# Splitting the scale weights by columns and reordering the text work in a dual-stream attention block

## Chip, cores and metric

The kernel runs on one core of a Trainium2 chip. The metric is the device time of one execution in microseconds. Weights and activations are bfloat16, sums float32.

## The reference

Two streams share one attention: 2 x 256 image tokens and 2 x 32 text tokens of width D = 1152. A conditioning vector c gives each stream a shift, a scale and a gate.

```python
mod_i = (_silu(c) @ wmod_img).reshape(B, 6, 1, D)      # likewise mod_t from wmod_txt
shi, sci, gai = mod_i[:, 0], mod_i[:, 1], mod_i[:, 2]
hi = _layernorm(x_img) * (1 + sci) + shi
ht = _layernorm(x_txt) * (1 + sct) + sht
qkvi, qkvt = hi @ wqkv_img, ht @ wqkv_txt              # each cut into q, k, v of width D
q, k, v = (concatenate([text, image], axis=1) ...)
p = _softmax(einsum('bqd,bkd->bqk', q, k) * D ** -0.5)
a = einsum('bqk,bkd->bqd', p, v)                       # one head of width D
at, ai = a[:, :Nt], a[:, Nt:]
out_i = x_img + gai * (ai @ wo_img)
out_t = x_txt + gat * (at @ wo_txt)
```

Of the six parts of each modulation, the first three are used. With all weights, the kernel reads 39.5 MB.

## The kernel before

**Tiles and loads.** A weight matrix of 1152 x 1152 lies in SBUF as nine blocks of 128 rows (`KT` = 9). Five slots hold such matrices; a slot is loaded again once its last reader is done. SP's queue issues nearly all loads in the program's order: x, the image scale weights `w_sc_i` by rows 0-3, 4-6, 7, 8 (line 108), the V weights `w_v_i` by rows (line 110), shift, q, text shift, k, text scale, text q and k. Behind the k stage's third hook come the late loads (`late_loads`, line 567): the image gate, the shift's V rows, text V, wo_img in two parts, the text gate, wo_txt in three. `pin` keeps instructions in the order in which the program gives them, on their engine; all matmuls go through `mm` (line 61), all PE transposes through `tr` (line 64).

**The head.** While weights arrive, c goes through silu into the columns `sT`, and TensorE runs warm-up matmuls (`warm_up`). ScalarE sums two of the four image tiles of 128 tokens (`ln_sums`), VectorE takes the statistics of the other two (`ln_stats`). The normalised tiles `xn_i` are transposed on TensorE in groups of three row blocks into PSUM tiles `tp`, which `x_out` copies into `xT_i`. The image scale is formed twice: `sc_rows` makes all of it as rows, four column groups beside each other, in matmuls of 288 columns, and `sc_cols` transposes them on VectorE; `sc_first` makes block 0 as columns, with the weights as stationary operand and `sT` as two moving columns. `x_scale` writes the scaled `hS_i` block by block.

**V.** `v_open` accumulates V over the nine row blocks, 512 columns at a time: `A0` is batch 0, `A1` the first half of batch 1, and the keys (2, 1) and (3, 1) the rest. The order before is: blocks 0-2 of A0, blocks 0-2 of A1, blocks 3-6 of both, blocks 7-8 key by key, then (2, 1), the shift rows (`mod_rows_of`), then (3, 1), and the last 128 columns (`v_last`). V is computed from the scaled tokens; the part of V that comes from the shift (`shift_v_rows`) is added behind the attention.

**q, k and text.** VectorE and ScalarE apply scale and shift to `xT_i` (lines 357-364, then called `hT_i`). `qk_img` makes q and k: for each of nine column blocks j it accumulates nine matmuls of 512 columns, and ahead of chosen j it runs hooks with the text work. The text shift is summed on VectorE (`shift_part`, line 450).

**Attention and output.** Four score tiles for the image and one for the text, then the image gate (`img_gate`), then text V (`v_txt`), with the softmax on VectorE, ScalarE and GpSimd beside them. `p_transposes` transposes P on TensorE. `gate_row` sends the gate's rows to HBM and `img_gate_spread` brings them back to all partitions as `gb`. `out_img` makes one image tile of the output in chunks of 384 columns: nine matmuls, then VectorE multiplies by the gate (line 723) and adds x (line 724). Behind tile 1 come the text gate (`txt_gate`) and the text output (`out_txt`), behind tile 2 the text products and sums (`out_txt_store`, lines 746 and 747):

```python
    out_img(1, C3)
    txt_gate()
    txt = out_txt()
    out_img(2, C3)
    out_txt_store(txt)
    out_img(3, (CH, CH, 224, 160), parts=(2 * CH, D - 160, D))
```

Of the kernel before, what the change touches and what calls it, by code (L numbers as in the profile page):

```python
# [14 lines left out]
def kernel(  # L15
# [14 lines left out]
    nc = tc.nc  # L30
# [75 lines left out]
    SCC = (0, 4, 7, K8, KT)  # L106
    for r0, r1 in zip(SCC, SCC[1:]):
        nc.sync.dma_start(w_sc_i[:, r0:r1, :], sc_v[:, r0:r1, :])  # L108
    for r0, r1 in ((0, 1), (1, 2), (2, 3), (3, 5), (5, 7), (7, KT)):
        nc.sync.dma_start(w_v_i[:, r0:r1, :], v_v[:, r0:r1, :])  # L110
    w_sh_i = load_w(2, wmod_img, 0)
    w_q_i = load_rows(3, wqkv_img, 0)
    w_sh_t = load_rows(0, wmod_txt, 0, (0, 1, 3, 6))
# [10 lines left out]
    nc.vector.memset(warm[:], 1.0)  # L124
    NGG = 4
# [7 lines left out]
    def warm_up(n):  # L133
        for _ in range(n):
            mm(wps[:], lhsT=warm[:, 0:P], rhs=warm[:], start=True, stop=True)

    warm_up(8)
# [27 lines left out]
    warm_up(14)  # L165
# [15 lines left out]
    def ln_stats(x_ap, np_, between=None):  # L181
        stats = small.tile([P, NCH, 6], f32, tag="stats")
        for k in range(NCH):
            if k == 1 and between:
                between()
            pin(nc.vector.bn_stats(stats[0:np_, k, :], x_ap[:, k * CH:(k + 1) * CH]))
        mv = small.tile([P, 2], f32, tag="mv")
        pin(nc.vector.bn_aggr(mv[0:np_, :], stats[0:np_, :, :]))
        return mv
# [34 lines left out]
    sc0_ps = ps_mm.tile([P, B], f32, tag="mm")  # L224
    tp60 = ps_mm.tile([P, 3, NI], bf, tag="mm", name="tp")
    tp61 = ps_mm.tile([P, 3, NI], bf, tag="mm", name="tp")
    sc_ps = ps_mm.tile([P, KT, LW], f32, tag="mm")

    def sc_first(r0, r1):
        if r0 == 0:  # L230
            mm(sc0_ps[:], lhsT=warm[:, 0:P], rhs=unit[:, 0:B], start=True, stop=False)
        for kt in range(r0, r1):
            mm(sc0_ps[:], lhsT=w_sc_i[:, kt, 0:P], rhs=sT[:, kt, :], start=False, stop=(kt == KT - 1))

    def sc_rows(r0, r1):
        if r0 == 0:
            for g in range(NGG):
                mm(sc_ps[LW * g:LW * g + LW].rearrange("p c l -> p (c l)"), lhsT=unit[:], rhs=warm[:, 0:KT * LW],
                   start=True, stop=False, tile_position=(0, LW * g))
        for kt in range(r0, r1):  # L240
            for g in range(NGG):
                mm(sc_ps[LW * g:LW * g + LW], lhsT=sT32[:, kt, :], rhs=group(w_sc_i, kt, g),
                   start=False, stop=(kt == KT - 1), tile_position=(0, LW * g))

    def x_tiles(k0, b):
        return (tp61 if b else tp60) if k0 == 6 else ps_tr.tile([P, 3, NI], bf, tag="tr", name="tp")

    def x_transposes(tp, k0, b, ts=range(TPB)):
        for kt in range(k0, k0 + 3):
            for t in ts:  # L250
                i = b * TPB + t
                tr(tp[:, kt - k0, t * P:(t + 1) * P], xn_i[:, i, kt * P:(kt + 1) * P], ident[:])

    def x_out(tp, k0, b):
        dst = xT_i[:, k0:k0 + 3, b * NI:(b + 1) * NI]
        pin(nc.vector.tensor_copy(dst, tp[:]) if k0 == 3 else nc.scalar.copy(dst, tp[:]))

    sc1_i = const.tile([P, KT, LW], f32, name="scc", tag="scc")

    def sc_cols(c0, c1):  # L260
        pin(nc.vector.transpose(sc1_i[:, c0:c1, :].rearrange("p c l -> p (c l)"),
                                sc_ps[:, c0:c1, :].rearrange("p c l -> p (c l)")))

    def x_scale(k0, k1, b, step=TPB, first=False):
        for kt in range(k0, k1):
            for t in range(0, TPB, step):
                t0, t1 = b * NI + t * P, b * NI + (t + step) * P
                pin(nc.vector.tensor_scalar(hS_i[:, kt, t0:t1], xT_i[:, kt, t0:t1],  # L268
                                            sc0_ps[:, b:b + 1] if first else sc1_i[:, kt, b:b + 1], None,
                                            op0=ALU.mult))  # L270
# [27 lines left out]
    m1 = ln_stats(x_i[:, 1, :], P, between=silu_cols)  # L298
# [3 lines left out]
    tps = [(x_tiles(k0, 0), k0, 0) for k0 in (3, 0, 6)]  # L302
    for tp in tps:
        x_transposes(*tp)
    s2 = ln_sums(x_i[:, 2, :], xn_i[:, 2, :])
    m3 = ln_stats(x_i[:, 3, :], P)
    ln_var(s2)
    x_out(*tps[0])
    r3, r2 = ln_rstd(m3[:, 1:2], P), ln_rstd(s2[:, 2:3], P, sign=-1.0)
    ln_norm(x_i[:, 3, :], m3[:, 0:1], r3, P, xn_i[:, 3, :])  # L310
    ln_norm(x_i[:, 2, :], s2[:, 0:1], r2, P, xn_i[:, 2, :])
    x_out(*tps[1])
    x_out(*tps[2])
    sc_rows(0, 4)
    sc_first(0, 4)
    warm_up(2)
    t3, t0, t6 = [(x_tiles(k0, 1), k0, 1) for k0 in (3, 0, 6)]
    x_transposes(*t3, ts=(1,))
    x_transposes(*t6, ts=(1,))
    sc_rows(4, 7)  # L320
    sc_first(4, 7)
    x_transposes(*t3, ts=(0,))
    x_transposes(*t6, ts=(0,))
    x_transposes(*t0)
    x_out(*t3)
    x_out(*t6)
    x_out(*t0)
    sc_first(7, K8)
    sc_first(K8, KT)
    sc_rows(7, KT)  # L330
    x_scale(0, 1, 0, step=1, first=True)
    sc_cols(0, 5)
    x_scale(1, 3, 0)
    v_open(A0, 0, 3)
    x_scale(0, 3, 1)
    sc_cols(5, KT)
    for k0 in (3, 6):
        for b in range(B):
            x_scale(k0, k0 + 3, b)
    v_open(A1, 0, 3)  # L340
    v_open(A0 + A1, 3, KT - 2)
# [10 lines left out]
    v_open([(2, 1)], 0, KT)  # L352
    p_sh = mod_rows_of(w_sh_i, sT32)
# [11 lines left out]
    v_open([(3, 1)], 0, KT)  # L365
# [15 lines left out]
    def qk_img(wq, blk, hooks):  # L381
        for j in range(KT):
            for hook in hooks.get(j, ()):
                hook()
            ps = ps_mm.tile([P, B * NI], f32, tag="mm")
            for kt in range(KT):
                mm(ps[:], lhsT=wq[:, kt, j * P:(j + 1) * P], rhs=hT_i[:, kt, :],
                   start=(kt == 0), stop=(kt == KT - 1))
            qk_evac(qkT[:, blk * KT + j, :, 0:NI], ps[:].rearrange("p (b n) -> p b n", b=B), blk)

    gsc = tc.dram_tile([2, B, D], bf, name="mod_scratch")
# [141 lines left out]
    def mod_row_out(gps, si):  # L533
        g_sb = work.tile([P, VC], bf, tag="garow")
        pin(nc.scalar.copy(g_sb[:], gps[:]))
        for b in range(B):
            pin(nc.gpsimd.dma_start(gsc[si, b, :].rearrange("(g j) -> g j", g=NGG), g_sb[b:P:32, :]))
# [15 lines left out]
    def txt_gate():  # L553
        mod_row_out(mod_rows(w_ga_t), 1)
        for g in range(2):
            pin(nc.gpsimd.dma_start(xf[64 * g:64 * g + NTT, :, :],
                                    xt_flat.rearrange("t (r g j) -> g t r j", r=2, g=2)[g]))
        for g in range(2):
            for b in range(B):
                r0 = 64 * g + 32 * b  # L560
                pin(nc.gpsimd.dma_start(gbf[r0:r0 + NT, :, :],
# [5 lines left out]
    def late_loads():  # L567
        late["ga_i"] = load_w(0, wmod_img, 2 * D)
        shift_v_spread()
        late["v_t"] = load_w(2, wqkv_txt, 2 * D)  # L570
# [5 lines left out]
                      5: (shift_part(4, 7),), 8: (shift_part(7, KT),)})  # L576
    qk_img(w_k_i, 1, {1: (txt_transposes,), 2: (shift_v_rows, txt_rows_scale, late_loads), 4: (shift_blocks, txt_scale),
# [100 lines left out]
    img_gate()  # L678
# [19 lines left out]
    gate_row()  # L698
# [8 lines left out]
    p_out(1, pt1, nc.scalar.copy, 1, B)  # L707
    img_gate_spread()
# [3 lines left out]
    def out_img(i, chunks, parts=None):  # L712
# [4 lines left out]
        for n in chunks:  # L717
# [33 lines left out]

    C3 = (CH, CH, CH)
    out_img(0, C3)
    out_img(1, C3)
    txt_gate()
    txt = out_txt()
# [33 lines left out]
```

## Time and profile before

| | |
|---|---|
| median of 14 runs | 117.24 us (116.55 to 119.75) |
| the profiled execution's own time | 117.85 us |
| its span | 115.8 us |
| TensorE busy | 110.1 us (95%) |
| VectorE busy | 72.3 us (62%) |
| ScalarE busy | 46.0 us (40%) |
| GpSimd busy | 13.2 us (11%) |
| moved by DMA | 41.02 MB, 354 GB/s over the span |

Times inside the kernel are counted from the span's start. In the profile PE is TensorE's matmuls, PEld its weight loads, DVE VectorE, ACT ScalarE, POOL GpSimd, SP SyncE. A line of the timeline gives start, length, engine, source line, operation, out<-in, shape and count; in brackets stands the idle time before it and what ended it. Consecutive instructions of one kind are merged, and the length of merged ones reaches from the first start to the last end. Matmuls are pipelined: each is shown some 0.16 us longer than its place in the stream. The share of busy time is a mean over stages with different limits.

### The profile page before, as it was taken

To read this page: it belongs to the slowest core of one execution; us is meant where nothing else is said; L and a number is where in the kernel's file an instruction comes from. 1 tells how busy PE (TensorE), PEld (TensorE's weight loads), DVE (VectorE), ACT (ScalarE), POOL (GpSimd) and SP (SyncE) were. 2 spreads that over 40 slices of the span, in tenths; PEclk is the share of its full clock that TensorE was granted. 3 is DMA by queue.
4 is the path that set the end of the run, shared out by engine and by line. 5 is a ranking of instruction groups with operands and counts; after the bars stand their busy time and mean duration, and the time that the engine had idled before them with its cause. 6 is when DMAs were issued, how large, how long until landed. Compare 5 with 4: busy or idle time off the path is not lost.

```text
span 115.8 us, 2644 instructions
## 1 busy us (share of the span) xinstructions
PE 110.1 (95%) x1109; PEld 63.2 (55%) x1109; DVE 72.3 (62%) x151; ACT 46.0 (40%) x97; POOL 13.2 (11%) x33
## 2 busy tenths in 40 slices
PE   4999899999999999999999999999999999999990
PEld 2245544444574444444744458887666566676670
DVE  3479494044799997999998040018758608904791
ACT  4799710032562369994323223244637500010000
POOL 7000000000000000000000000003440300068130
PEclk9999999999999999999999999999999999999999
DMA  3999999999999999999999999999999999952143
GB/s 127 369 350 382 400 401 408 416 409 410 413 405 404 319 382 409 410 409 326 395 399 408 411 404 415 351 404 408 411 405 409 408 416 409 406 205 76 26 135 120
DMA packets 18917, 41.02 MB, mean 354 GB/s; under 512 B 1323, under 2 KB 1851, under 8 KB 18907
## 3 DMA queue, kind: packets, MB, share of 16 engines
q1 hardware_dynamic: 18032, 39.85, 90.1%
q0 software_dynamic: 480, 0.89, 2.3%
q10 hardware_dynamic: 395, 0.12, 0.5%
q8 instruction: 8, 0.13, 0.4%
q14 instruction: 2, 0.02, 0.0%
HBM read 39.52 MB, written 1.34 MB: 353 GB/s over the span
## 4 chain that ended last, share of the span: by engine, by line
PE 68%; DMA 22%; DVE 4%; SPq 2%; issue 1%; DVEq 0%
PE ps L61 40%; PE vps L61 15%; DMA t<-in_wqkv_txt_dram 13%; DMA t<-in_wmod_img_dram 9%; PE aps L61 5%; PE gps L61 4%; PE txo L61 2%; DVE tmp L723 2%; SPq L108 2%; DVE o L724 2%; PE pT_ps L64 1%; SPq L104 1%; DVE tmp L746 1%; DVE hS_i L268 0%; PE sc_ps L61 0%
## 5 line engine op out<-in xcount | busy, mean ns | idle before, releaser
L61 PE MATMUL ps<-xT_i,t 128*128 128x512 bf16 x162 | 35.5, 379 | 0.0
L61 PEld LDWEIGHTS <-t 128*128 128x128 bf16 x333 | 21.0, 98 | 19.4 <-issue 0.5
L450 DVE SCALAR_TENSOR_TENSOR acc_sh<-t,sTf,acc_sh 128x1152 f32<-128x1152 bf16 x16 | 21.4, 1409 | 0.0
L61 PE MATMUL vps<-t,hS_i 128*128 128x512 bf16 (+1 forms) x108 | 17.9, 326 | 0.2 <-DVE hS_i L268 0.2
L61 PE MATMUL ps<-t,aT 128*128 128x384 bf16 (+2 forms) x117 | 17.9, 314 | 0.0
L61 PEld LDWEIGHTS <-aT 128*128 128x128 bf16 (+1 forms) x189 | 13.1, 97 | 6.9 <-issue 0.2
L61 PEld LDWEIGHTS <-hS_i 128*128 128x128 bf16 x108 | 9.1, 98 | 8.9 <-DVE hS_i L268 0.4
L723 DVE TENSOR_TENSOR tmp<-ps,gb 128x384 bf16<-128x384 f32 (+2 forms) x13 | 6.8, 522 | 9.0 <-PE ps L61 5.1
L379 ACT CAST qkT<-ps 128x512 bf16<-128x512 f32 (+2 forms) x11 | 6.1, 552 | 14.1 <-PE ps L61 12.8
L611 POOL TENSOR_SCALAR pb<-e,rs 128x32 bf16<-128x32 f32 (+1 forms) x5 | 2.3, 459 | 75.8 <-DVE rs L603 75.8
L61 PE MATMUL wps<-warm 128*128 128x512 bf16 x24 | 7.9, 487 | 1.5 <-DVE unit L128 1.5
L176 DVE CAST v_i<-vps 128x512 bf16<-128x512 f32 x5 | 3.5, 692 | 8.0 <-PE vps L61 8.0
L377 ACT ACTIVATE qkT<-ps 128x512 bf16<-128x512 f32 (+2 forms) x11 | 5.8, 562 | 5.9 <-PE ps L61 5.9
L591 DVE TENSOR_REDUCE nmx<-sps 128x1 f32<-128x288 f32 x4 | 1.8, 458 | 9.4 <-PE sps L61 9.4
L178 ACT CAST v_i<-vps 128x512 bf16<-128x512 f32 x4 | 2.3, 581 | 10.4 <-PE vps L61 10.4
L61 PEld LDWEIGHTS <-sT 128*32 128x32 bf16 x180 | 4.6, 96 | 2.0 <-issue 1.3
L61 PEld LDWEIGHTS <-warm 128*128 128x128 bf16 x25 | 2.7, 116 | 5.2 <-issue 2.6
L61 PE MATMUL sps<-qkT 128*128 128x288 bf16 (+1 forms) x54 | 5.3, 287 | 0.0
L724 DVE TENSOR_TENSOR o<-tmp,x_i 128x384 bf16<-128x384 bf16 (+2 forms) x13 | 5.0, 381 | 0.4
L61 PE MATMUL gps<-t,sT 128*32 128x288 bf16 x144 | 5.2, 287 | 0.0
L656 DVE TENSOR_SCALAR aT<-aps,svc 128x288 bf16<-128x288 f32 x9 | 4.3, 518 | 1.4 <-PE aps L61 1.4
L61 PE MATMUL aps<-pT,v_i 128*128 128x288 bf16 x36 | 5.1, 287 | 0.0
(110 smaller groups left out, 110.5 us busy)
## 6 DMA issues: line engine op xcount, KB each, us to landing
t<-in_wqkv_txt_dram SPq DMA_DIRECT2D x3, 2592.0 KB, 11.8
t<-in_wmod_img_dram SPq DMA_DIRECT2D x2, 2592.0 KB, 15.4
t<-in_wmod_txt_dram SPq DMA_DIRECT2D x2, 2592.0 KB, 21.3
t<-in_wqkv_img_dram SPq DMA_DIRECT2D x3, 864.0 KB, 14.3
t<-in_wqkv_img_dram SPq DMA_DIRECT2D x1, 2592.0 KB, 16.6
t<-in_wqkv_img_dram SPq DMA_DIRECT2D x3, 576.0 KB, 8.5
t<-in_wmod_txt_dram SPq DMA_DIRECT2D x2, 864.0 KB, 13.0
t<-in_wo_img_dram SPq DMA_DIRECT2D x1, 1440.0 KB
```

The lines of the kernel that those rows point to most:

```text
L61: return pin(nc.tensor.matmul(*a, **k))
L108: nc.sync.dma_start(w_sc_i[:, r0:r1, :], sc_v[:, r0:r1, :])
L176: nc.vector.tensor_copy(out_ap, in_ap)
L178: nc.scalar.copy(out_ap, in_ap)
L377: nc.scalar.mul(out_ap, in_ap, SCALE)
L379: nc.scalar.copy(out_ap, in_ap)
L450: pin(nc.vector.scalar_tensor_tensor(acc, w_sh_t[:, kt, :], col, acc, op0=ALU.mult, op1=ALU.add))
L591: pin(nc.vector.reduce_max(nmx[0:qn, :], sps[0:qn, :], axis=AX.X, negate=True))
L611: pin(nc.gpsimd.tensor_scalar(dst, src, rs[0:qn, :], 0.0, op0=ALU.mult, op1=ALU.add))
L656: nc.vector.tensor_scalar(dst, tiles[(b, dt)][:], bias, None, op0=ALU.add)
L723: pin(nc.vector.tensor_mul(tmp[:, 0:n], ps[:, 0:n], gb[:, b, c0:c0 + n]))
L724: pin(nc.vector.tensor_add(o[:, c0:c0 + n], tmp[:, 0:n], x_i[:, i, c0:c0 + n]))
```

## The change

- The scale weights are loaded in two column halves: columns 0-639 (five blocks, `SA` = 5) by rows 0-3, 4-7, 8, then V rows 0 to 4 one by one, then columns 640-1151 by rows 0-4 and 5-8, then the other V rows. The text shift weights come in three parts instead of four.
- The scale is made as columns alone (`sc_mm`), 45 matmuls of two columns for half a and 36 for half b, each half with an opening matmul. The rows, their transposes and `sc_first` go.
- The transposes of batch 0 follow the first 20 column matmuls; those of batch 1 come between the V matmuls. V opens with blocks 0-3 of A0, then block 4, then blocks 0-4 of A1, then the rest. VectorE's statistics of tile 3 are cut by hooks (`between` is a table now) that copy and scale the first blocks.
- (3, 1) comes ahead of the shift rows.
- `qk_img` takes `lead`: for q the first three column blocks run together, row block by row block up to the sixth. The k hooks 2 and 4 become 3 and 5.
- Text V is loaded ahead of the image gate. The gate's matmuls and rows move behind the transposes of P and their copies.
- The text gate and output run behind two chunks of image tile 2, the text store behind one chunk of tile 3. The text gate's rows go out on ACT's queue and come back on SP's; the text x rows are loaded behind tile 0.
- Warm-ups are f32: 2 and 3 instead of 8 and 14, and the pair in the head goes.

```diff
-    SCC = (0, 4, 7, K8, KT)
-    for r0, r1 in zip(SCC, SCC[1:]):
-        nc.sync.dma_start(w_sc_i[:, r0:r1, :], sc_v[:, r0:r1, :])
-    for r0, r1 in ((0, 1), (1, 2), (2, 3), (3, 5), (5, 7), (7, KT)):
+    SA = 5
+    for r0, r1 in ((0, 4), (4, K8), (K8, KT)):
+        nc.sync.dma_start(w_sc_i[:, r0:r1, 0:SA * P], sc_v[:, r0:r1, 0:SA * P])
+    for r in range(SA):
+        nc.sync.dma_start(w_v_i[:, r:r + 1, :], v_v[:, r:r + 1, :])
+    for r0, r1 in ((0, SA), (SA, KT)):
+        nc.sync.dma_start(w_sc_i[:, r0:r1, SA * P:D], sc_v[:, r0:r1, SA * P:D])
+    for r0, r1 in ((5, 6), (6, 7), (7, KT)):
         nc.sync.dma_start(w_v_i[:, r0:r1, :], v_v[:, r0:r1, :])
...
-    w_sh_t = load_rows(0, wmod_txt, 0, (0, 1, 3, 6))
+    w_sh_t = load_rows(0, wmod_txt, 0, (0, 1, 4))
...
+    def sc_mm(ps, c0, c1, r0, r1):
         if r0 == 0:
-            mm(sc0_ps[:], lhsT=warm[:, 0:P], rhs=unit[:, 0:B], start=True, stop=False)
...
+            mm(ps[:].rearrange("p c b -> p (c b)"), lhsT=warm[:, 0:P], rhs=unit[:, 0:(c1 - c0) * B],
+               start=True, stop=False, skip_group_check=True)
+        for c in range(c0, c1):
+            for kt in range(r0, r1):
+                mm(ps[:, c - c0, :], lhsT=w_sc_i[:, kt, c * P:(c + 1) * P], rhs=sT[:, kt, :],
+                   start=False, stop=(kt == KT - 1), skip_group_check=True)
...
+    sc_mm(sc_a, 0, SA, 0, 4)
+    tps = [(tp, k0, 0) for tp, k0 in zip(tp_b0, (0, 3, 6))]
+    for tp in tps[0:2]:
         x_transposes(*tp)
+    sc_mm(sc_a, 0, SA, 4, K8)
+    sc_mm(sc_a, 0, SA, K8, KT)
+    x_transposes(*tps[2])
     s2 = ln_sums(x_i[:, 2, :], xn_i[:, 2, :])
...
+    def first_scales():
+        x_scale(0, 1, 0, col=sc_a[:, 0, 0:1], step=1)
+        pin(nc.vector.tensor_copy(sc1_i[:, 0:SA, :], sc_a[:]))
+        x_scale(1, 3, 0)
+        ln_var(s2)
+
+    m3 = ln_stats(x_i[:, 3, :], P, between={1: lambda: x_out(*tps[0]), 2: first_scales})
+    x_out(*tps[1])
+    r2 = ln_rstd(s2[:, 2:3], P, sign=-1.0)
+    x_out(*tps[2])
+    r3 = ln_rstd(m3[:, 1:2], P)
+    x_scale(3, SA, 0)
+    ln_norm(x_i[:, 2, :], s2[:, 0:1], r2, P, xn_i[:, 2, :])
     ln_norm(x_i[:, 3, :], m3[:, 0:1], r3, P, xn_i[:, 3, :])
...
+    v_open(A0, 0, 4)
+    t0, t3 = [(ps_tr.tile([P, 3, NI], bf, tag="tr", name="tp"), k0, 1) for k0 in (0, 3)]
+    for t in range(TPB):
+        x_transposes(*t0, ts=(t,))
+        x_transposes(*t3, ts=(t,))
+    x_out(*t0)
     x_out(*t3)
+    x_scale(0, SA, 1)
+    v_open(A0, 4, SA)
+    v_open(A1, 0, 3)
+    sc_b = ps_tr.tile([P, KT - SA, B], f32, tag="tr")
+    sc_mm(sc_b, SA, KT, 0, SA)
+    v_open(A1, 3, SA)
+    sc_mm(sc_b, SA, KT, SA, KT)
+    x_scale(SA, SA + 1, 0, col=sc_b[:, 0, 0:1])
+    pin(nc.vector.tensor_copy(sc1_i[:, SA:KT, :], sc_b[:]))
+    t6 = (ps_tr.tile([P, 3, NI], bf, tag="tr", name="tp"), 6, 1)
+    x_transposes(*t6)
     x_out(*t6)
...
+    v_open(A0 + A1, SA, KT - 2)
     v_open(A0 + A1, KT - 2, KT, kt_major=False)
...
     v_open([(2, 1)], 0, KT)
+    v_open([(3, 1)], 0, KT)
     p_sh = mod_rows_of(w_sh_i, sT32)
...
+    def qk_img(wq, blk, hooks, lead=1):
+        for j0, j1 in [(0, lead)] + [(j, j + 1) for j in range(lead, KT)]:
+            for hook in hooks.get(j0, ()):
                 hook()
+            ps = [ps_mm.tile([P, B * NI], f32, tag="mm", name="ps") for j in range(j0, j1)]
+            for k0, k1 in ((0, K6), (K6, KT)):
+                for kt, j in [(kt, j) for kt in range(k0, k1) for j in range(j0, j1)] if k0 == 0 else \
+                        [(kt, j) for j in range(j0, j1) for kt in range(k0, k1)]:
...
     def late_loads():
+        late["v_t"] = load_w(2, wqkv_txt, 2 * D)
         late["ga_i"] = load_w(0, wmod_img, 2 * D)
         shift_v_spread()
-        late["v_t"] = load_w(2, wqkv_txt, 2 * D)
...
     st = scores_txt()
-    img_gate()
     vt = [v_txt(0)]
...
-    gate_row()
     v_txt_out(0, vt[0])
...
     p_out(1, pt1, nc.scalar.copy, 1, B)
+    img_gate()
+    gate_row()
     img_gate_spread()
...
     out_img(0, C3)
+    txt_x()
     out_img(1, C3)
-    txt_gate()
-    txt = out_txt()
-    out_img(2, C3)
-    out_txt_store(txt)
-    out_img(3, (CH, CH, 224, 160), parts=(2 * CH, D - 160, D))
+    out_img(2, C3, hooks={2: txt_run})
+    out_img(3, (CH, CH, 224, 160), parts=(2 * CH, D - 160, D), hooks={1: lambda: out_txt_store(txt)})
```

`txt_run` is the text gate and then the text output; `txt_x` holds the two loads of text x rows that stood in `txt_gate`.

## The prediction

> **What bounds the kernel now.** I read the chain of waits first, then the timeline of the three places that the change touches (the head, the softmax, the tail), then the queue totals.
>
> ```profile
> 3.59 10.30 DMA t<-in_wmod_img_dram
> ...
> 14.22 0.44 DVE hS_i L268 x2
> 14.66 13.74 PE vps L61 x63
> 28.40 1.22 PE gps L61 x36
> 29.61 4.06 PE vps L61 x45
> 33.67 21.37 PE ps L61 x99
> ...
> 66.97 15.33 DMA t<-in_wqkv_txt_dram
> ...
> 82.35 2.39 PE ps L61 x72
> ```
>
> Columns: start, length, what. Up to 13.9 us the chain is the load of the scale weights; from 14.66 TensorE runs without a hole to 82 us, where it meets the load of the text V weights; then TensorE again to the end. So time is won only by starting V earlier, by removing the wait at 82, or behind the last matmul.
>
> ```profile
> 10.19 0.67 PE L61 MATMUL sc_ps<-t,sT 128*32 128x288 bf16 x16 [0.16 <-DMA t<-in_wmod_img_dram]
> 10.84 0.24 PE L61 MATMUL sc_ps<-sT,t 128*128 128x2 bf16 x4
> 12.33 0.55 PE L61 MATMUL sc_ps<-t,sT 128*32 128x288 bf16 x12 [0.24 <-DMA t<-in_wmod_img_dram]
> 12.90 0.83 PE L64 MATMUL tp<-ident,xn_i 128*128 128x128 bf16 x12
> 13.93 0.18 PE L61 MATMUL sc_ps<-sT,t 128*128 128x2 bf16 x1 [0.20 <-DMA t<-in_wmod_img_dram]
> 14.22 0.43 DVE L268 TENSOR_SCALAR hS_i<-xT_i,sc_ps 128x128 bf16<-128x128 bf16 x2 [0.40 <-PE sc_ps L61]
> ```
>
> The head's timeline: rows 0-3 of the scale weights land at 10.2, 4-6 at 12.3, the last at 13.9, so one row of 288 KB takes (13.93 - 10.19)/5 = 0.75 us. From the last column matmul (13.93) to the first V matmul (14.64) are 0.71 us. Four column matmuls take 0.24 us and one 0.163, so they start (0.24 - 0.163)/3 = 0.026 us apart; transposes likewise (0.83 - 0.219)/11 = 0.056. All 36 transposes lie in this waiting time.
>
> ```profile
> 80.70 1.38 PE L61 MATMUL gps<-t,sT 128*32 128x288 bf16 x36
> 82.35 2.39 PE L61 MATMUL ps<-t,hT_t 128*32 128x288 bf16 x72 [0.27 <-DMA t<-in_wqkv_txt_dram]
> 83.33 0.36 DVE L605 TENSOR_SCALAR pb<-e,rs 64x288 bf16<-64x288 f32 x1
> 84.67 1.01 PE L64 MATMUL pT_ps<-ident,pb 128*128 128x128 bf16 x15
> ```
>
> The softmax: the scores' issue ends at 80.6, the gate fills 1.2 us, text V waits some 0.4 us for its weights. The text rows of P are ready at 83.69, 3.1 us after the scores: hidden now, since the transposes begin at 84.67.
>
> ```profile
> 109.16 0.82 DVE L746 TENSOR_TENSOR tmp<-txo,gbf 128x288 bf16<-128x288 f32 x2
> 109.69 1.42 POOL L747 TENSOR_TENSOR of<-tmp,xf 128x288 bf16<-128x288 bf16 x2 [2.59 <-DVE tmp L746]
> 110.47 0.85 DVE L724 TENSOR_TENSOR o<-tmp,x_i 128x384 bf16<-128x384 bf16 x1
> 111.83 0.36 DVE L724 TENSOR_TENSOR o<-tmp,x_i 128x384 bf16<-128x384 bf16 x1
> 112.71 0.32 DVE L723 TENSOR_TENSOR tmp<-ps,gb 128x160 bf16<-128x160 f32 x1
> ```
>
> The tail: the two text products cost VectorE 0.73 us before the next one starts, and while GpSimd adds (1.42 us) an image add takes 0.85 instead of 0.36. Four pieces follow, so VectorE is in step again at the end.
>
> ```profile
> q1 hardware_dynamic: 18032, 39.85, 90.1%
> q10 hardware_dynamic: 395, 0.12, 0.5%
> ```
>
> Packets, MB, share of 16 engines' 115.8 us: 92.6 ns for a mean packet of 2210 B, 23 ns for 304 B. By the line through both, a packet of 2304 B takes 96 ns, of 1280 B 59, of 1024 B 49: a split row costs 1.12 of a whole one.
>
> **The change part by part.**
>
> *Half a of the scale (640 columns).* Up to 10 us the queues move 0.35-0.36 MB/us, so the four rows took 1.18/0.357 = 3.3 us; in 640 columns 0.61 x 3.3 = 2.0, so they land at 8.9. Rows 4-7 follow in 1.9 (10.8), row 8 at 11.25, V row 0 at 12.0. On TensorE 20 column matmuls at 10.8 (0.5 us) and 5 more end at 11.4; plus 0.71, V starts at 12.1 instead of 14.64: **-2.5 us**. V rows then land each 0.75 us, under the 0.86 that four matmuls of 0.2155 take.
>
> *What moves behind V's start.* 37 column matmuls of half b x 0.026 = 0.96, and the 18 transposes of batch 1 x 0.056 = 1.0: **+2.0 us** on TensorE, which no longer waits there.
>
> *New waits on VectorE.* Its queue now holds bn_stats, the variance and the LayerNorms of tiles 2 and 3 between the scalings. Blocks 0-3 of batch 0 are fed in time (scaled at 12.4, 12.7, 12.9, 14.2; used at 12.1 + 0.86 each). LayerNorm of tile 3 ends near 15.5, when TensorE is done with four blocks. Then A1's first matmul needs: transposes (16.2), their copy (0.55), one scaling (0.27), 0.2 of handover: 17.4, against 17.1 when block 4 of A0 is done: 0.3. Block 5 needs half b's last matmul (20.4), 0.29 to VectorE, a scaling, 0.2: 21.2, against 20.8: 0.4. **+0.7 us** (bounds 0 and 1.5: everything hidden, or both waits doubled). Queued behind are scalings for blocks that TensorE needs later. The scale's two transposes (0.34, 0.31) become copies of some 0.2.
>
> Sum of the head: -2.5 + 2.0 + 0.7 = **+0.2 us** where q begins.
>
> *Costed at nothing.* Warm-ups in f32: no f32 matmul is in the trace. Nearest row: eight bf16 ones in 3.60 us. If f32 cost the same, 2 + 3 would be a quarter of the warming; [...] the wait for half a (8.9) covers either, and without that cover 0.5 us. The (3,1) block ahead of the shift rows takes 1.94 us of cover from the shift of hT (12 VectorE operations over 3.2 us); v_last (2.2 us) is left, hT's block 0 is ready 1.3 us after the rows, a block follows each 0.35 us, and key-major use takes 0.65 a block. In block order it would be some 1 us. The split rows delay all later loads by 9 x 0.12 x 0.75 = 0.8 us, and the hooks stand one block (1.9 us) later: the fold (67.0) has its input at 62.0. Text k's load issues 1.9 us later than its 56.3 and takes 11.8, so it lands at 70 and is used at 73.3.
>
> *Text V ahead, gate behind the transposes.* Text V changes places with a load of 2.65 MB, 6.5 us at 0.41 MB/us, so it lands near 76 and the 0.4 wait goes. But gate and wait covered the softmax. Now: scores end, text V 2.3 us, two transposes, then the third waits for the text rows of P (3.1 + 0.1 after the scores); 13 transposes 0.73, gate 1.3: attention starts 5.25 after the scores instead of 85.53 - 80.58 = 4.95: **+0.3 us**. The gate's rows reach GpSimd 3 us later; gb then lands near 99 instead of 95.7. Six PSUM tiles last TensorE to 91.6 + 6 x 1.47 = 100.4, so it is covered by 0.8 us. The text x rows' two GpSimd issues (0.6 each) follow gb's, where nothing waits behind them.
>
> *The tail.* Text gate and text output move behind two chunks of image tile 2, the text products behind the first chunk of tile 3. The gate's row goes out on ACT's queue (two issues of some 0.6) and comes back on SP's (four of 0.45, landing 2 us): about 6 us after the gate's end. SP has only the store of tile 1 ahead, done by then, and the store of tile 2 behind. TensorE fills 2.3 + 1.47 + 1.47 and VectorE 1.0, so the products start in time by about 0.6. But now pieces of 384, 224 and 160 columns follow, one of 384 less: 0.73 + 0.49 meet 0.6 of slack. VectorE's tmp for the 224-column piece starts 0.77 after its matmul instead of 0.14: **+0.6 us** (0 if GpSimd does not slow it, 1.3 if the row lands late).
>
> Sum: 0.2 + 0.3 + 0.6 = +1.1 on the profiled execution's own 117.85, 118.95. It lies 0.6 above the median of 117.24, so I forecast **118.3**.
>
> **The rivals.**
>
> *Clock.* [...] Row first:
>
> ```profile
> 8.60:14.64 6.04, 5.22 (x89) 3.50 (x89) 4.23 (x12) 5.10 (x12) 0.00 (x0) 1.00 1.03 391
> ```
>
> The granted clock is 1.00 here with 36 transposes, but also with 40 matmuls of 288 and two of 512 columns, which the change replaces by matmuls of 2. By the row nothing; [...] Chance 0.09.
>
> *The head pays in full.* TensorE's work from 8.6 to 33.67 at its spacings is 23.0 us, so 2.1 us are idle. If the column matmuls and transposes fall into waits and VectorE keeps ahead, q begins up to 2 us earlier. The sum is 0.9 less this gain; it is faster than now by over 0.35 once q begins 1.3 us earlier (before 32.4). At 1.7: 116.4. For it: 2.1 idle. Against: waits for half a at 8.9 and 10.8 and the 0.71 turnaround stay. Chance 0.23.
>
> *The change does not reach the end:* a head gain of 0.6 to 1.3 is returned at softmax and tail: 117.2, chance 0.13.
>
> **How the numbers follow.** My case (0.55): 117.7 to 119.2. Clock 0.09, head 0.23, no effect 0.13. 0.3% (0.35 us) is about what a measurement of this kernel can tell from none. Slower: 0.55 + 0.09 = 0.64; same 0.13; faster 0.23. The range 116.7 to 119.4 leaves out most of the clock case and half of the head case.
>
> **What would show it.** V's first matmul near 12.1; no wait longer than 0.5 before 34; the first q matmul within 0.7 of 33.8; a wait of 0.6 inside the 15 transposes on P; no wait for text V; gb landing at 98-100; text products some 3.3 us before the last VectorE operation ends (4.2 now). I am wrong if q begins before 32.5, if the transposes on P do not wait, or if the clock drops.

## Result and profile after

| | before | after |
|---|---|---|
| median, us | 117.3 (47 runs, 116.55 to 119.75) | 118.85 (10 runs, 118.62 to 118.97) |
| profiled execution, us | 117.85 | 118.88 |
| its span, us | 115.8 | 117.1 |
| first V matmul | 14.64 | 12.10 |
| first q matmul (by the chain of waits) | 33.67 | 33.38 |
| scores' last matmul ends | 80.98 | 80.69 |
| attention's last matmul ends | 91.49 | 91.45 |
| last VectorE operation ends | 113.31 | 113.80 |
| last store lands | 114.88 | 116.12 |

The change makes the kernel slower: the ratio is 1.0132 (95% interval 1.011 to 1.0153). The rows from "first V matmul" on are from the two traces. The differences between them carry 1.24 of the 1.55 us between the medians: V starts 2.54 us sooner, q only 0.29 us sooner; attention gives those 0.29 back (-0.04 is left), the last VectorE operation is 0.49 later, and the last store 1.24 later. The ratios leave out executions more than 1.5% above the fastest of their kernel; the profiles of two experiments below (tail_back, gate_between) are of such executions.

The chain of waits after (start, length, what):

```profile
3.44 8.62 DMA t<-in_wqkv_img_dram
12.10 3.61 PE vps L61 x16
15.71 0.67 PE tp L64 x12
16.38 2.28 PE vps L61 x10
18.66 0.50 PE sc_b L61 x21
19.16 0.89 PE vps L61 x4
20.05 0.38 PE sc_b L61 x16
20.42 0.36 PE tp L64 x6
...
33.38 23.31 PE ps L61 x108
```

The early start is real: the load that frees V (V's own first row here, the last row of the scale before) ends at 12.06 instead of 13.9. But from 12.10 on the chain is TensorE alone, and half b of the scale (`sc_b`, 0.50 + 0.38) and the transposes of batch 1 (0.67 + 0.36), which before lay in the wait ahead of V, now lie between V's matmuls: 1.91 us by the chain.

The timeline of the head, with what each instruction waited for in brackets:

```profile
9.27 0.65 PE L61 MATMUL sc_a<-sT,t 128*128 128x2 bf16 x20 [0.23 <-DMA t<-in_wmod_img_dram]
...
10.92 0.78 PE L61 MATMUL sc_a<-sT,t 128*128 128x2 bf16 x25 [0.31 <-DMA t<-in_wmod_img_dram]
...
17.18 0.98 PEld L61 LDWEIGHTS <-hS_i 128*128 128x128 bf16 x6 [0.43 <-DVE hS_i L256]
...
20.81 0.11 PEld L61 LDWEIGHTS <-hS_i 128*128 128x128 bf16 x2 [0.20 <-DVE hS_i L256]
```

These are the only two waits for VectorE behind V's start, at the two places where the prediction put them (A1's first matmul, block 5). They are waits of the weight load. At the first of them the load had run ahead of the matmuls: two V matmuls start 0.32 us apart there instead of 0.216, so 0.11 of the 0.43 us reaches TensorE. At the second, behind the short transposes, nearly all does: the next matmul starts 0.25 us after the last transpose instead of 0.056, so 0.19 of 0.20. From the first V matmul to the first q matmul are 21.28 us instead of 19.03, that is 2.25 more: 1.9 of moved work and 0.3 of these waits. The 2.25 is the same in every trace: counted to q's own first start, V to q is 21.12 to 21.14 us in all nine traces with this head and 18.87 to 18.89 in the four with V as in the kernel before.

The timeline of the softmax:

```profile
80.41 2.49 PE L61 MATMUL ps<-t,hT_t 128*32 128x288 bf16 x72
82.83 0.28 PE L64 MATMUL pT_ps<-ident,pb 128*128 128x128 bf16 x2
83.45 0.90 PE L64 MATMUL pT_ps<-ident,pb 128*128 128x128 bf16 x13 [0.34 <-DVE pb L606]
84.28 1.29 PE L61 MATMUL gps<-t,sT 128*32 128x288 bf16 x36
85.50 0.66 PE L61 MATMUL aps<-pT,v_i 128*128 128x288 bf16 x4
```

Text V follows the scores with no wait, two transposes run, and the third waits for the text rows of P. Attention starts 4.81 us after the scores' end (85.50 - 80.69); before it was 4.55 (85.53 - 80.98).

The timeline of the tail, VectorE, GpSimd and the queues of SP and ScalarE together:

```profile
110.51 0.82 DVE L749 TENSOR_TENSOR tmp<-txo,gbf 128x288 bf16<-128x288 f32 x2
111.05 1.41 POOL L750 TENSOR_TENSOR of<-tmp,xf 128x288 bf16<-128x288 bf16 x2 [16.32 <-DVE tmp L749]
...
112.49 0.61 SPq L753 DMA_DIRECT2D out_dram<-of  x1
113.15 1.08 SPq L730 DMA_DIRECT2D out_dram<-o  x2
113.56 0.24 DVE L727 TENSOR_TENSOR o<-tmp,x_i 128x160 bf16<-128x160 bf16 x1
113.83 0.39 ACTq L730 DMA_DIRECT2D out_dram<-o  x1
```

The text products start 3.29 us before the last VectorE operation ends (4.15 before). The text stores go out at 112.49 instead of 111.14, 1.35 us later, and directly ahead of the last image stores. What that does is seen in the table by windows. Its columns are the window, its length, the busy time of TensorE, its weight load, VectorE, ScalarE and GpSimd (instructions in brackets), the granted clock, the mean busy share of the 16 DMA engines, and GB/s. After:

```profile
113.50:114.00 0.50, 0.00 (x0) 0.00 (x0) 0.27 (x2) 0.00 (x0) 0.00 (x0) 1.00 0.36 88
114.00:114.50 0.50, 0.00 (x0) 0.00 (x0) 0.00 (x0) 0.00 (x0) 0.00 (x0) 1.00 0.98 234
114.50:115.00 0.50, 0.00 (x0) 0.00 (x0) 0.00 (x0) 0.00 (x0) 0.00 (x0) 1.00 1.01 363
115.00:115.50 0.50, 0.00 (x0) 0.00 (x0) 0.00 (x0) 0.00 (x0) 0.00 (x0) 1.00 0.73 195
```

and before:

```profile
112.50:113.00 0.50, 0.16 (x3) 0.00 (x0) 0.48 (x2) 0.00 (x0) 0.00 (x0) 1.00 0.95 227
113.00:113.50 0.50, 0.00 (x0) 0.00 (x0) 0.27 (x2) 0.00 (x0) 0.00 (x0) 1.00 0.99 325
113.50:114.00 0.50, 0.00 (x0) 0.00 (x0) 0.00 (x0) 0.00 (x0) 0.00 (x0) 1.00 0.76 229
114.00:114.50 0.50, 0.00 (x0) 0.00 (x0) 0.00 (x0) 0.00 (x0) 0.00 (x0) 1.00 0.34 82
```

The DMA shares add up to the same work: (0.36 + 0.98 + 1.01 + 0.73) x 0.5 = 1.54 us of all 16 engines after, (0.95 + 0.99 + 0.76 + 0.34) x 0.5 = 1.52 before. Before, this pile begins while VectorE still works on the last pieces (0.97 us of it is done by 113.5), and the share is down to 0.76 and 0.34 in the microsecond from 113.5 on: the last store to land (ScalarE's, 40 KB) is issued at 113.34 and lands at 114.88, after 1.54 us. After, the pile begins when VectorE is nearly done (0.18 us of it by 114.0), and the last one to land (SP's, 56 KB), issued at 113.83, takes 2.29 us; the store of the same piece took 1.53 before.

### The profile page after: what moved, and what is told of

Its sections match the earlier page's. It is cut to its first block, busy times and chain, and to the rows that moved or that the text cites. A ratio compares the mean times of both kernels' runs of the same rounds, so it can differ in the third digit from the quotient of the medians.

```text
span 117.1 us, 2683 instructions
## 1 busy us (share of the span) xinstructions
PE 109.6 (94%) x1128; PEld 63.8 (54%) x1128; DVE 72.3 (62%) x152; ACT 46.5 (40%) x97; POOL 10.0 (9%) x27
## 3 DMA queue, kind: packets, MB, share of 16 engines
HBM read 39.52 MB, written 1.34 MB: 349 GB/s over the span
## 4 chain that ended last, share of the span: by engine, by line
PE 81%; DMA 7%; DVE 5%; SPq 2%; ACT 1%; issue 1%; DVEq 0%
PE ps L61 47%; PE vps L61 15%; DMA t<-in_wqkv_img_dram 7%; PE gps L61 5%; PE aps L61 5%; PE sps L61 4%; PE txo L61 2%; SPq L108 1%; DVE tmp L726 1%; DVE o L727 1%; PE tp L64 1%; PE pT_ps L64 1%; PE sc_b L61 1%; DVE tmp L749 1%; SPq L104 1%
## 5 line engine op out<-in xcount | busy, mean ns | idle before, releaser
L61 PEld LDWEIGHTS <-t 128*128 128x128 bf16 x405 | 22.9, 97 | 20.4 <-DMA t<-in_wmod_img_dram 1.2
L61 PE MATMUL vps<-t,hS_i 128*128 128x512 bf16 (+1 forms) x108 | 18.5, 326 | 0.1
L61 PE MATMUL wps<-warm 128*128 128x512 f32 x10 | 7.0, 841 | 2.0 <-DVE unit L134 2.0
L534 ACT CAST g_sb<-gps 128x288 bf16<-128x288 f32 x2 | 0.8, 398 | 13.1 <-PE gps L61 13.1
L250 ACT COPY xT_i<-tp 128x768 bf16<-128x768 bf16 x4 | 3.2, 789 | 5.5 <-PE tp L64 5.5
L61 PE MATMUL ps<-hT_t,t 128*128 128x64 bf16 x162 | 5.1, 193 | 0.0
```

The source lines that it names most:

```text
L61: return pin(nc.tensor.matmul(*a, **k))
L250: pin(nc.vector.tensor_copy(dst, tp[:]) if k0 == 0 else nc.scalar.copy(dst, tp[:]))
```

## The experiments

The times of one group are of one chip, beside runs of the kernel before on it: a median of 116.88 us for tail_back, gate_between, head_alone and tail_alone; 117.05 for after_again, of_pool, best and best_b; 117.23 for tail_early, part_early and split_only. "End to store" below is the time from the end of the last VectorE operation to the last landing; before has 1.57, after 2.32. In all seven traces in which the text stores are issued 2.17 us ahead of VectorE's end it is 1.57 to 1.59; in the four in which they are issued 1.3 us ahead, with nothing else changed in the stores, it is 2.30 to 2.33.

### The second half: tail_alone, tail_back, head_alone, gate_between

tail_alone is the kernel before with the end of the kernel after:

```diff
-    out_img(1, C3)
-    txt_gate()
-    txt = out_txt()
-    out_img(2, C3)
-    out_txt_store(txt)
-    out_img(3, ...)
+    txt_x()
+    out_img(1, C3)
+    out_img(2, C3, hooks={2: txt_run})
+    out_img(3, ..., hooks={1: lambda: out_txt_store(txt)})
```

(with the gate's row on ScalarE's and SP's queues, as in the change).

> The kernel before with the end of the changed one alone (places and queues of text gate, text output and text store). Theory: VectorE ends 0.5 us later and the last stores land 0.7 us later still: 118.4 to 118.6. Rival: the end costs nothing, 117.3.

Measured: 118.23 us, ratio 1.0108 (1.0076 to 1.014). From the end of attention to the last VectorE operation 22.34 us (before 21.82, after 22.35), end to store 2.32. So the end alone brings 0.52 + 0.75 = 1.27 us, nearly the whole loss. This trace also has before's first half without a wait for text V:

```profile
80.18 1.39 PE L61 MATMUL gps<-t,sT 128*32 128x288 bf16 x36
81.29 2.49 PE L61 MATMUL ps<-t,hT_t 128*32 128x288 bf16 x72
...
84.56 0.91 PE L61 MATMUL aps<-pT,v_i 128*128 128x288 bf16 x6
```

Attention starts 4.09 us after the scores' end (80.47), against 4.55 in before's profiled execution. The wait for text V is thus not in every execution of that order.

tail_back is the other way round, the kernel after with before's order of calls:

```diff
-    out_img(2, C3, hooks={2: txt_run})
-    out_img(3, ..., hooks={1: lambda: out_txt_store(txt)})
+    txt_run()
+    out_img(2, C3)
+    out_txt_store(txt)
+    out_img(3, ...)
```

> The changed kernel with the text gate and text output behind image tile 1 again and the text store behind tile 2 (the ACT and SP queues for the text gate stay). If the loss sits in the order at the end (0.5 us on VectorE plus 0.7 us in the last stores), the end comes earlier by 1.2 us, less a wait of text output for the last rows of wo_txt, which land near 103.9 and are wanted near 103.1: 118.0 to 118.3. If the order at the end costs nothing and the loss sits before it: 118.8.

Measured: ratio 1.0112 (1.0072 to 1.0152), a miss. End to store is 1.58, as before, so the late stores are gone. But the theory had put the wait for wo_txt at some 0.8 us, and the timeline shows more:

```profile
102.34 2.07 PE L61 MATMUL txo<-t,aT 128*32 128x288 bf16 x56 [1.05 <-DMA t<-in_wo_txt_dram]
106.06 0.67 PE L61 MATMUL txo<-t,aT 128*32 128x288 bf16 x16 [1.65 <-DMA t<-in_wo_txt_dram]
```

In this profiled execution the text output waits 2.7 us for the parts of wo_txt. How long the wait is in its other executions is not shown. It ran at a granted clock of 1.00, so such waits belong to this kernel, and the ratio flatters it: the median of all ten executions is 119.06 us. The trace says that the place of the text output and the place of the text store have to be told apart: the first covers a load, the second costs.

head_alone keeps the head of the change, and the late loads, hooks, gate and end of before:

```diff
-        late["v_t"] = load_w(2, wqkv_txt, 2 * D)
         late["ga_i"] = load_w(0, wmod_img, 2 * D)
         shift_v_spread()
+        late["v_t"] = load_w(2, wqkv_txt, 2 * D)
...
-    img_gate()
-    gate_row()
     img_gate_spread()
```

(here against the kernel after; gate and gate row back at before's places.)

> The changed kernel with late loads, hooks of k, place of the image gate and end as before the change: the head alone. Theory: q begins 0.3 us earlier than in the kernel before, but all loads land some 0.8 us later, so text V is awaited about 1.2 to 1.5 us instead of 0.4: 117.9 to 118.3. Rival, the head pays: 117.0 or less.

Measured: 117.55 us, ratio 1.005 (1.003 to 1.007). As a time this lies between theory and rival; over the 116.88 of the kernel before on this chip it is 0.6 to 0.7 us more, the lower end of what the theory adds to 117.3. V starts at 11.86 and q at 33.15, 21.29 us apart; tail_alone, with before's head, has 14.12 and 33.16. Between these two traces the head brings q nothing. The loads behind it land later, and head_alone's trace meets text V's weights late, so that attention starts 4.71 us after the scores' end, 0.62 later than in tail_alone:

```profile
81.98 2.39 PE L61 MATMUL ps<-t,hT_t 128*32 128x288 bf16 x72 [0.42 <-DMA t<-in_wqkv_txt_dram]
```

gate_between is the kernel after with the image gate between text V and the transposes of P:

```diff
     vt.append(v_txt(1))
+    img_gate()
+    gate_row()
     pt0, pt1, pt2 = p_transposes(0, ps_tr), ...
...
-    img_gate()
-    gate_row()
     img_gate_spread()
```

> The changed kernel with the image gate's matmuls between text V and the transposes of P. If the gate only lost its place as cover of the softmax, the wait inside the transposes (0.3 to 0.5 us) goes and attention starts near 84.9 instead of 85.5: 118.1 to 118.3. If the transposes wait for something else, or the image gate's weights (landing near 81.9) come too late: 118.8 or more.

Measured: ratio 1.0094 (1.0073 to 1.0114), 0.4% under the kernel after, as the theory had it (the two intervals just touch). In the profiled execution, though, the gate waited itself:

```profile
83.68 1.29 PE L61 MATMUL gps<-t,sT 128*32 128x288 bf16 x36 [1.06 <-DMA t<-in_wmod_img_dram]
```

With text V loaded first, the gate's weights land last: at 81.9 in the profile of the kernel after, at 83.6 here. The order has little room.

### Gate and store taken apart: after_again, best, best_b, tail_early

after_again is the kernel after once more, as the measure for its group.

> The changed kernel as it is, so that the other kernels of this group stand beside it on one chip. Expected: 1.3% over the kernel before, last stores landing about 2.3 us after the last VectorE operation ends, the two products of the text rows on VectorE within 4 us of the end.

Measured: 118.51 us, ratio 1.0138 (1.0114 to 1.0162); end to store 2.30, text products 3.29 us before the last VectorE operation ends. best changes three places of it:

```diff
-    out_img(1, C3)
-    out_img(2, C3, hooks={2: txt_run})
-    out_img(3, ..., hooks={1: lambda: out_txt_store(txt)})
+    out_img(1, C3, hooks={2: txt_gate})
+    out_img(2, C3, hooks={2: lambda: txt.extend(out_txt())})
+    out_txt_store(txt)
+    out_img(3, ...)
```

and the gate as in gate_between.

> The changed kernel with three places of its second half changed: the image gate between text V and the transposes of P (not behind them), the text gate inside image tile 1 (not tile 2), and the text store back behind image tile 2 (not inside tile 3); the text products stay inside tile 2. Theory: this takes away the late VectorE products and late stores (1.2 us) and the softmax wait (0.4 us), while the text output weights still have their time to land: 117.0 to 117.5 us, ratio 0.998 to 1.003, which leaves the head as worth about nothing. Rival (the head itself costs, as head_alone's 1.005 might be read): ratio 1.005 or more.

Measured: 117.09 us, ratio 1.0009 (0.9989 to 1.0028). The whole loss is gone with the head of the change still in place. The timeline of its softmax:

```profile
80.01 2.49 PE L61 MATMUL ps<-t,hT_t 128*32 128x288 bf16 x72
82.22 1.39 PE L61 MATMUL gps<-t,sT 128*32 128x288 bf16 x36
83.54 1.01 PE L64 MATMUL pT_ps<-ident,pb 128*128 128x128 bf16 x15
84.39 0.91 PE L61 MATMUL aps<-pT,v_i 128*128 128x288 bf16 x6
...
86.21 1.02 PE L61 MATMUL aps<-pT,v_i 128*128 128x288 bf16 x7 [0.32 <-ACT aT L659]
```

No wait for text V, none inside the transposes; attention starts 4.09 us after the scores' end (80.30), and then gives some of it back at a wait for ScalarE that the kernel after does not have (attention takes 6.44 us here, 5.95 there). End to store is 1.57.

tail_early has the text calls of best and leaves the gate behind the transposes.

> The changed kernel with the text gate inside image tile 1, the text products inside tile 2, and the text store behind tile 2 (as in `best`), but with the image gate still behind the transposes of P. Theory (1.2 us of the loss come from the late text store and 0.5 to 0.7 from the gate's place): attention still starts about 4.8 us after the scores' end, the last store lands 1.6 us after the last VectorE operation; 117.5 to 117.8 us, ratio 1.004 to 1.006. Rival (the two losses are one, since gb lands late behind the gate and drags the end): 1.009 or more.

Measured: 117.53 us, ratio 1.0028 (1.0009 to 1.0047): 1.1% under the kernel after, for the same first half (attention starts 4.81 us after the scores' end, as there). Its stores are issued at before's distances:

```profile
111.13 0.62 SPq L753 DMA_DIRECT2D out_dram<-of  x1
112.21 0.94 SPq L730 DMA_DIRECT2D out_dram<-o  x2
```

SP's text store is done 0.46 us before the next image store, and end to store is 1.58. Text gate, text products and store moved forward thus take away 1.3 us of 1.6. The gate's place brings some 0.2 more (best): 0.24 us from the scores' end to attention's end in the traces, while the intervals of the two ratios overlap. That is less than the theory's 0.5 to 0.7, since best has the wait for ScalarE in its place.

best_b is the second half of best on the kernel before; it differs from best in the head alone (to which `lead` and the places of the k hooks are counted).

```diff
+        late["v_t"] = load_w(2, wqkv_txt, 2 * D)
         late["ga_i"] = load_w(0, wmod_img, 2 * D)
         shift_v_spread()
-        late["v_t"] = load_w(2, wqkv_txt, 2 * D)
```

(against before; gate and text calls as in best.)

> The kernel before with the same second half as the kernel `best` (text V loaded and multiplied ahead of the image gate, gate between text V and the transposes of P, text gate inside image tile 1, text products inside tile 2, store behind tile 2). Only the head differs between the two. Theory (the head is worth nothing net, and before waits 0.3 to 0.4 us for text V's weights, which is gone here): within 0.2% of `best`, ratio 0.996 to 0.999. Rival (the head's extra packets delay the later loads and so cost): 0.4% or more below `best`.

Measured: 116.88 us, ratio 0.9988 (0.9968 to 1.0007). In the traces V starts 2.56 us apart (best 11.70, best_b 14.26), q 0.31 apart (32.99 and 33.30). By the times best lies 0.2% above best_b, and the intervals overlap: the head is worth nothing that these runs can tell from zero. The traces show where its 0.31 us went: at the scores' end best is still 0.30 ahead (80.30 against 80.60), but the wait for ScalarE stands in best's attention and not in best_b's, which ends first (90.66 against 90.83). Why best has that wait is open. best_b is the fastest kernel of this study; that it beats the kernel before is not shown.

### What makes the last stores late: of_pool, part_early

of_pool sends the text stores through GpSimd's queue:

```diff
-            eng = nc.sync if g == 0 else nc.scalar
+            eng = nc.gpsimd
```

> The changed kernel, with the two stores of the text rows on GpSimd's queue instead of SP's and ScalarE's. Theory (SP's text store of 0.61 us stands ahead of the two image stores that end the run, and is what makes them late): the image stores are issued 0.6 us sooner and the end comes 0.4 to 0.6 us earlier, ratio about 1.008 to 1.010. Rival (the stores are late because four of them are in flight within 1.4 us, whoever issues them): GpSimd's stores are issued at much the same time, the end does not move by more than 0.2 us, ratio 1.012 or more.

Measured: ratio 1.016 (1.0133 to 1.0188), no gain from freeing SP's queue. Its image stores were indeed issued sooner,

```profile
112.26 0.94 SPq L730 DMA_DIRECT2D out_dram<-o  x2
112.32 1.19 POOL L753 DMA_DIRECT2D out_dram<-of  x2 [0.29 <-POOL of L750]
```

1.10 us before the last VectorE operation ends (113.36), where the kernel after has 0.65. SP's last packets move before 114.75, but ScalarE's image store still has packets until 115.25, 1.89 us behind VectorE's end (after: 1.81 to the last packet). The landing of the image stores is not in this trace; GpSimd's second text store lands at 115.49, 2.13 behind. The table by windows from 113 us on has DMA shares of 0.73, 1.16, 0.49, 0.83 and 0.10, a pile of 1.66 us. The test is not a clean one: GpSimd issues its two stores one behind the other, the second at 112.87 where the kernel after has both out at 112.50, so SP's queue is freed at the price of a later text store.

part_early lets a part of the pile go ahead:

```diff
-    out_img(3, (CH, CH, 224, 160), parts=(2 * CH, D - 160, D), ...)
+    out_img(3, (CH, CH, 224, 160), parts=(CH, 2 * CH, D - 160, D), ...)
```

> The changed kernel with one store more: image tile 3's first 384 columns are stored as soon as they are ready, instead of together with the next 384. Theory (at the end the DMA engines have a pile of 432 KB to drain, at 0.96 to 1.00 busy for 1.5 us; 96 KB of it can go 1.3 us sooner): the pile is shorter by 0.3 us, last landing about 2.0 us after the last VectorE operation, ratio 1.010 to 1.012. Rival (what counts is the time from issue to landing of one store, or the extra store costs SP's queue 0.4 us): no change, ratio 1.013 or more.

Measured: ratio 1.0207 (1.0151 to 1.0264). In the trace the pile is shorter as expected (shares 0.61, 1.00, 0.85, 0.19 from 113.5 us on: 1.33 us), and end to store is 2.11 instead of 2.32. The run is not shorter. Two of the six executions took 120.7 us at granted clocks of 0.980 and 0.983, and they are in the ratio; the other four, at 0.990 or more, took 118.97 to 119.21, still some 1.6% above the kernel before. In the trace the span ends 1.4 us after the last landing, where the kernel after has 1.0; where that comes from no line of the profile shows. So pile and last landing move together in the traces, but a gain in time is shown only for moving the text work as a whole (tail_early, best).

### What a later V start costs: split_only

split_only is the kernel before with its scale loads cut by columns:

```diff
-    SCC = (0, 4, 7, K8, KT)
-    for r0, r1 in zip(SCC, SCC[1:]):
-        nc.sync.dma_start(w_sc_i[:, r0:r1, :], sc_v[:, r0:r1, :])
+    for r0, r1 in ((0, 4), (4, KT)):
+        for c0, c1 in ((0, 640), (640, D)):
+            nc.sync.dma_start(w_sc_i[:, r0:r1, c0:c1], sc_v[:, r0:r1, c0:c1])
```

> The kernel before, with its four scale loads cut by columns instead of rows alone: rows 0-3 and 4-8, each as 640 and 512 columns. As many DMAs and bytes as before; only the packets differ (twice as many, of 1280 and 1024 bytes in place of 2304). Theory (the split rows cost 1.1 us of transfer, and V's start is followed by a TensorE that is full up to q): V starts 1.1 us later, at 15.2 to 15.8, and the end comes 0.7 to 1.1 us later, ratio 1.006 to 1.010. Rival (packets of this size cost nothing, or the later waits for weights swallow it): V starts within 0.3 us of before, or the end moves by less than 0.3%.

Measured: ratio 1.0143 (1.0086 to 1.02); it holds one execution of 119.99 us at a granted clock of 0.985, and the three at 0.996 or more took 118.31 to 118.62, 1.1 to 1.4 us above the 117.23 of the kernel before. The slowdown came, and only a part of its reason. The last piece of the scale lands at 13.97 us, against 13.89 in before's trace. But the same whole rows land at 13.37 in tail_alone, so one execution of before is no measure. The DMA view from 9 to 12 us, split_only first, tail_alone second, gives packets, MB and busy share:

```profile
q1 hardware_dynamic: 914, 1.04, 103.4%
q1 hardware_dynamic: 569, 1.21, 103.8%
```

At the same busy share 14% fewer bytes moved. The records of single packets from 6 to 14 us have a median of 93 ns for 2304 bytes, 55 for 1280 and 46 for 1024: 101 ns for a split row in place of 93, 9% more, where the prediction reckoned 12%. Over nine rows of 0.75 us that is an estimate of 0.6 us, as much as lies between 13.97 and 13.37. The edit changed a second thing, which its expectation overlooked, the groups of rows, and V starts late for that reason too:

```profile
14.01 0.55 PE L61 MATMUL sc_ps<-t,sT 128*32 128x288 bf16 x12 [1.86 <-DMA t<-in_wmod_img_dram]
...
14.59 0.83 PE L64 MATMUL tp<-ident,xn_i 128*128 128x128 bf16 x12
...
15.37 0.43 PE L61 MATMUL sc_ps<-t,sT 128*32 128x288 bf16 x8
15.88 4.49 PE L61 MATMUL vps<-t,hS_i 128*128 128x512 bf16 x20
```

Before, rows 4-6 came at 12.3 and only the last of the scale was left behind the last landing; here rows 4-8 came together, and their matmuls and twelve transposes stand behind it: 1.91 us from landing to V, against 0.75. This makes it the counterpart of the change. V starts 1.24 us later (15.88), q 1.26 later (34.93), the scores end 1.26 later (82.24): V's later start was passed on in full where the work of TensorE behind it stayed the same. The last VectorE operation ends only 0.73 later than in before's trace, since text V does not wait here (attention starts 4.10 us after the scores' end, against 4.55).

## Why the prediction was right, and where it was not

The sum of the prediction was +1.1 us. The measured difference is 1.55 us between the medians, 1.03 between the two profiled executions, and 1.24 at the last landing in their traces. That the sum came so near has luck in it: the head came out 0.49 us better than predicted (-0.29 instead of +0.2), and the landing of the last stores, which the prediction did not cost, 0.75 us worse. Step by step:

**V's start: right.** Predicted 12.1, measured 12.10. That it is exact is chance: the other eight traces with this head have 11.65 to 11.97, and three with before's head 14.12 to 14.64. A lead of some 2.5 us holds in all of them.

**What moves behind it: right.** Predicted 2.0; the chain shows 1.91 in four pieces. Every trace with this head has the same 2.25 us more from V to q, whenever V starts, and split_only shows that an equal shift of V without moved work goes through to the scores in full, so 2.25 of the 2.54 us were lost to the moved work and its waits, and not to something later.

**VectorE waits: mis-sized.** They are the two predicted, but 0.3 together instead of 0.7. The first was added up wrongly: 16.2 + 0.55 + 0.27 + 0.2 is 17.2 and not 17.4, which leaves 0.1 behind the 17.1, and 0.11 was measured. The second was put at 0.4 and cost 0.19. With them the head comes to -0.29 in the trace instead of +0.2. The times do not confirm a gain: best against best_b gives +0.2%, not told from zero.

**Split rows: about right.** V's last row lands 0.84 us later than before (21.29 against 20.45), predicted 0.8 for the loads behind the split; over all traces it is 20.95 to 21.57 with this head and 20.22 to 20.66 with before's. The price per packet, read from a line through two queues' means, was 12% for a split row, and the packet records have 9%. split_only, with the same packets and no DMA more, has V's last row at 20.76, only 0.1 to 0.5 later than whole rows. What makes up the rest was not tried; the change also issues three loads more there (13 against 10).

**Softmax: right.** Predicted +0.3; the time from the scores' end to attention's end goes from 10.51 to 10.76. The wait inside the transposes is 0.34 on TensorE, 0.51 at its weight load (predicted 0.6), text V does not wait, and gb lands at 97.8 and 99.3 (predicted near 99) and is covered. The gain that was counted here, the wait for text V, belongs to the profiled execution and not to the kernel: tail_alone has before's order with no such wait and 10.05. So the loss against an execution without the wait is 0.71 (10.76 against 10.05), and the medians differ by more than the two profiled executions do (1.03).

**Tail: right, and short of one step.** Predicted +0.6 on VectorE, measured 0.53 (22.35 against 21.82), and 0.52 in tail_alone. Missing is the step behind it: the prediction ended at the last VectorE operation and took the stores' landing as a constant. The text store moved with the text products, 1.35 us later, its traffic fell on that of the last image stores, and the last landing came another 0.75 us later. The shares by window show it, tail_alone brings it to the kernel before, and tail_early takes it away again; of_pool frees SP's queue without a gain, though with a later second text store.

**Rivals.** The rival by the clock, a V that starts slower, was the author's supposition and no trace here shows it; in the profiled execution it fell. But the row of before on which the prediction relied is a weak witness, because the same column reads 1.00 where matmuls of 512 columns start twice as far apart as later ones. From the kernel before, a row of the table and the warm-ups of the same time, and from the kernel after the start of V:

```profile
2.00:4.00 2.00, 2.00 (x7) 0.62 (x6) 0.20 (x2) 1.57 (x4) 0.82 (x3) 1.00 0.94 365
1.46 3.60 PE L61 MATMUL wps<-warm 128*128 128x512 bf16 x8 [1.46 <-DVE unit L128]
12.10 3.61 PE L61 MATMUL vps<-t,hS_i 128*128 128x512 bf16 x16
```

The eight warm-ups start 0.427 us apart, the V matmuls of the same size 0.216, from the first one on. That is the better evidence: V began at the spacing of its later matmuls, with the f32 warm-ups ending at 9 us and only matmuls of few columns and transposes in the 3.1 us from there. Nor is the rival out of every execution. Of the 121 executions of the eight kernels with this head, 15 had a mean granted clock of 0.980 to 0.986, though none of the kernel after itself, and most of these took 1.5 to 2.2 us longer than the median of their kernel's others; of the 125 of before, tail_alone and best_b beside these runs, none had; of split_only's six, with 1.86 us of waiting ahead of V, three had. In after's trace the column reads 0.50 from 115.9 to 117.0 us, where no engine and no DMA is busy; by an estimate from that value, a mean of 0.985 over 117 us is 3.5 us at 0.50. None of these executions was profiled, so where in them the clock was low is open. The head did not pay in full, and a gain did not merely fail to reach the end. The warm-ups in f32: two take 3.78 us where eight in bf16 took 3.60, 4.2 times as much for each. The last of them ends at 9.03 us, before half a lands (its first column matmul waits 0.23 us for the load and starts at 9.27), so the wait for half a covered them.

## What to carry to other kernels

An early start is worth little if it is bought by moving work from a wait into the stage that has none, here 0.3 us of 2.5: add up TensorE's busy time behind the start first. Follow a moved step to its last DMA: the store that went out 1.35 us later here cost 0.75 us at the end although VectorE's own step was costed rightly, since from 114.0 to 115.5 us the kernel after had no engine busy but those of the DMA, at shares of 0.98, 1.01 and 0.73. And look for the text or side work that can go earlier, not later: here the text gate, the text products and the text store, moved forward, gave back 1.1%. Compare several executions before a difference of half a microsecond between two traces is read as an effect: the same loads landed 0.5 us apart in two kernels with the same head.

## What the hardware showed that was not expected

- The final stores are 0.43 MB, and moving them took about 1.5 us of all 16 DMA engines (shares of 0.95 to 1.01 over a full microsecond, at 230 to 360 GB/s). A store of 56 KB landed after 2.3 us where the text stores had gone out 1.34 us ahead of it (after), and after 1.5 where they had gone out 1.69 ahead (before).
- One packet of 2304 bytes took 93 ns (median), one of 1280 bytes 55 and one of 1024 bytes 46, in the traces of before, after and split_only: cutting 288 KB rows of weights in two cost about 9% of packet time (101 ns in place of 93).
- A wait of 0.43 us at a weight load took only 0.11 us from TensorE, where loads ran ahead of long matmuls; one of 0.20 behind short transposes took 0.19.
- The column of the granted clock read 1.00 from 2 to 4 us, where matmuls of 512 columns started 0.427 us apart, twice the 0.216 of later ones. The spacing of equal matmuls was the better sign of TensorE's pace.
